# Set attention and a two-layer squared-ReLU network in one kernel: when a DMA may do an addition, when tokens are fetched, and rules for every four blocks

## The chip, the core and the metric

The kernel runs on one core of a Trainium2 chip. The metric is the device time of one execution in microseconds; less is better. TensorE (PE, with its weight loads shown apart as PEld), VectorE (DVE), ScalarE (ACT), GpSimd (POOL) and SyncE (SP, which here only issues DMAs) each run their own list of instructions in order and wait for one another by semaphores.

## What is computed

Four batches of 12480 tokens of width 128 attend to 32 inducing points, which have themselves attended to all tokens of their batch (`h`). The result goes through a network of width 2048 with `s * relu(h)^2 + b` between its layers.

```python
h = mab(I, x)                       # softmax(scale * I @ x.T) @ x, I is 32 x 128
x = mab(x, h).reshape(49920, 128)   # softmax(scale * x @ h.T) @ h
r = np.maximum(x @ w_in, 0.0)
return (s * (r * r) + b) @ w_out
```

## The kernel before, in words

Tokens stand in 104 blocks of 480 (26 for each of the four batches). A block passes through 8 pairs of hidden tiles (a pair is 2 x 128 hidden units, so its tiles are 128 x 960), which makes 832 pairs. A pair's work:

- PE: two matmuls h<-a2t,wst (`pair`, L988) of the block's attention weights with the weights that hold `h @ w_in`.
- ACT or DVE: r = relu(h) (L1000 on ACT, L1002 on DVE). The planner chooses.
- ACT: hi = the square of r, rounded to fp32r (`square`, L1062).
- PE: four matmuls of hi with w_lo and w_hi, summed into the block's output bank x (`out_part`, L1094).
- The rest that the rounding of hi lost, in one of three ways. **P**: DVE makes g = max(h,0)*r (L1031), POOL subtracts hi from it (L1042), and two matmuls with w_hi read that. **D**: DVE does both (L1031 into h, then L1042 on DVE). **Far**: DVE makes gm = -h*r (L1013), POOL issues a DMA that adds gm onto hi in memory (L1018; hi then has the home hm), and after it has landed two matmuls with w_neg = -w_hi read the sum. The four matmuls of hi must have read hm before that DMA may write it, and POOL waits for them.

So every pair costs PE the same eight matmuls, whichever way it goes.

Beside the pairs run chains of other steps, each beside a given block: `attend` (the attention of four blocks of tokens; one every fourth block, L838 to L876; it uses the output bank that the next block but one will need), and, except in the last batch, `scores`, `top` and `values` for the next batch's `h`. `attend` writes hl, from which SP's DMAs spread a2t for each block (L941). The tokens come in tiles xt of two blocks, two tiles to a group of four blocks, five buffers (`load_xt`, L359). `fetch` gives each load the block whose predecessor's output must have been made before it is issued (its gate, "ob"); both tiles of a group have had the same gate, two blocks ahead of their use (AHEAD = 2).

The order on every engine is written before the program runs, by a list scheduler (`Plan`). Each step has an engine or a choice of engines, a duration that the planner assumes, events that it waits for, and an urgency (the number of its pair, plus an offset from the rules: M_U for the first matmuls, R_U for the relu, OUT for the last matmuls, and so on); when engines come free, the step with the least start time plus WEIGHT times urgency is next. The durations are the planner's own: a far addition is taken to have landed M_LAND after POOL's issue, and a subtraction to take POOL_L on POOL. A pair goes far when this holds (M_PAIR is pairs 0 and 1 of a block, M_ROOM the two buffers of gm and hm):

```python
far = pr in (M_PAIR if steady else M_PAIR[:1]) and fars.get(k // NPAIR, 0) < M_MOST and blk_open(k)
far = far and max(next_free("gm", M_ROOM), next_free("hm", M_ROOM)) <= plan.end
```

`blk_open` asks whether the chain beside the block before has ended (in the plan) and the block before that has been written out; beside an attention it is mostly false when pairs 0 and 1 come. There are two sets of rules, `Opening` for pairs 0 to 15 and `Steady` for the rest, and `Steady` adds small offsets by the block's number in its batch and by pair.

Of the kernel before, what the change touches and what calls it, by code (L numbers as in the profile page):

```python
# [23 lines left out]
SB = 2  # L24
GR = 4
# [5 lines left out]
POOL_M = 0.6  # L31
M_LAND = 8.0
M_PAIR = (0, 1)
M_ROOM = 2
M_MOST = 1
G = 3
# [6 lines left out]
LAT = 0.195  # L43
IDLE = 0
BACK = 0.13
# [6 lines left out]
SETTLED = 16  # L52
END = 5
END_Q = 0.337
W_IN_U = -100
# [4 lines left out]
FRONT_0 = -9.51  # L60
# [22 lines left out]

class Opening:
    WEIGHT = 0.0229
    SLIP = 0.0865
    LEAN = {"ACT": -0.624}
    R_LEAN = {"DVE": 0.022}
    M_U = -8.4567
    R_U = 5.0037  # L90
    SQ = 2.0571
    S_U = -1.5635
    C_U = -15.3862
    OUT_HI = 2.8109
    OUT = 2.7863
    FRONT = -1.9358
    POOL_Q = 2.4761


class Steady:  # L100
    WEIGHT = 0.0178
    SLIP = 0.006
    LEAN = {'ACT': -0.624}
    R_LEAN = {'DVE': 0.021}
    M_U = -9.7754
    R_U = 4.4418
    SQ = 3.602
    S_U = -1.7977
    C_U = -16.8378
    OUT_HI = 2.732  # L110
    OUT = 2.166
    FRONT = -1.0039
    POOL_Q = 2.8611
    R_AT = [0.07, 0.0, 0.0, 0.0, 0.0, 0.0, 0.0, 0.0, 0.0, 0.0, 0.0, 0.02, 0.0, 0.0, 0.0, 0.0, -0.03, 0.0, 0.0, 0.0, 0.0, 0.0, -0.06, -0.0, 0.0, 0.0]
    Q_AT = [-0.01, 0.0, 0.0, 0.0, 0.0, 0.0, 0.16, 0.11, 0.01, 0.56, 0.17, 0.0, -0.18, 0.0, 0.58, 0.15, 0.0, 0.08, 0.0, -0.09, 0.0, 0.0, 0.0, 0.0, 0.0, 0.0]
    F_AT = [0.39, 0.0, 0.0, -0.12, 0.0, 0.0, 0.58, 0.0, -1.14, 1.46, 0.47, 0.52, 0.0, 0.0, 0.0, 0.0, -1.24, 0.0, 0.0, 0.0, -0.94, 0.0, 0.0, 0.0, 0.33, -0.95]
    R_PR = [0.03, 0.0, 0.0, -0.05, 0.01, 0.0, -0.07, 0.0]
    Q_PR = [-0.39, 0.53, 0.25, 0.19, 0.04, 0.0, 0.16, -0.35]

# [29 lines left out]
class Plan:  # L149
# [7 lines left out]
    def __init__(self):  # L157
        self.free, self.events, self.units, self.end, self.start = {}, Events(), [], 0.0, 0.0
        self.events[LOCK] = -math.inf
        self.pair_until = 0.0  # L160
        self.rules, self.lag = Opening, LAT

# [34 lines left out]
    def run(self):  # L197
        ev = self.events
        while self.units:
# [22 lines left out]
            self.units.remove(u)  # L222
            idle = self.eng == "PE" and self.rules is Steady and at > self.free.get("PE", 0.0) + 1e-6
            self.start, self.end = at, at + u[3][self.eng] + IDLE * idle
# [7 lines left out]
def tile_attn_relu2(ctx: ExitStack, tc: tile.TileContext, xT, xN, xF, indT, w_in, w_out, s_rep, b_rep, outT):  # L232
# [494 lines left out]
    def scores(b, g, ps, *waits):  # L727
# [17 lines left out]
        for q in range(nb):  # L745
            xt, turn = xt_tiles[b, (GR * g + q) // SB, 1]
            nc.tensor.matmul(ps[M * q:M * (q + 1), 0:BLK], ind_sb, xt[:, q % SB], start=True, stop=True)  # L747
            if q % SB == SB - 1:
                plan.set(turn)
        yield "DVE", 0.63  # L750
        nc.vector.tensor_tensor_reduce(
# [18 lines left out]
    def values(b, g, ps, *waits):  # L770
        d = st[b]
        rows = M * blocks_in(g)
        e = d["s"][0:rows, g]
        yield "ACT", 0.675, ("top", b), *waits
        nc.scalar.activation(
# [17 lines left out]
        plan.set(("eT", e_turn))  # L793
        yield "DVE", 0.29
        if g == 0:
# [179 lines left out]
    def pair(k):  # L975

        b, blk, pr = place(k)
        if k == SETTLED:
            plan.rules = Steady
        c, steady = plan.rules, plan.rules is Steady  # L980
        turn, free = ring("h", 3)
# [10 lines left out]
        if k + 1 < total:  # L992
            plan.spawn(pair(k + 1), k + 1, plan.end)
        lean = {"DVE": c.R_LEAN["DVE"] + c.R_AT[blk] + c.R_PR[pr]} if steady else c.R_LEAN
        yield dict(ACT=0.852, DVE=1.066), lean, c.R_U, room("r", RB)
# [8 lines left out]
        hi = {}  # L1004
        far = pr in (M_PAIR if steady else M_PAIR[:1]) and fars.get(k // NPAIR, 0) < M_MOST and blk_open(k)
        far = far and max(next_free("gm", M_ROOM), next_free("hm", M_ROOM)) <= plan.end
# [18 lines left out]
        wait = max(0.0, pool_work[0] - plan.end)  # L1025
        most = c.POOL_Q + (c.Q_AT[blk] + c.Q_PR[pr] if steady else 0.0) if k < total - END else END_Q
        kind = "P" if wait < most and next_free("g", G) <= plan.start else "D"
# [90 lines left out]
    def front_work(blk_g):  # L1118

        units = todo.pop(blk_g, [])  # L1120

        def ps():
            return bank[(blk_g + 1) % 2]

        def chain():
            first = True
            for f, args in units:
                for want in f(*args, ps):
                    yield (*want, ("ob", blk_g - 1), ("front", blk_g - 1)) if first and blk_g else want
                    first = False  # L1130
            plan.set(("front", blk_g))

        plan.spawn(chain(), blk_g * NPAIR + plan.rules.FRONT + (Steady.F_AT[blk_g % NBLK] if plan.rules is Steady else 0.0) if blk_g else FRONT_0, plan.end)

# [10 lines left out]
    for b in range(B):  # L1145
# [8 lines left out]
        for n, f, *args in sorted(units, key=lambda x: (x[0], rank.index(x[1]), x[2:])):  # L1154
            beside(at + n, f, *args)
            if f in (scores, attend):
                for j in range(args[1] * GR // SB, min(NSB, (args[1] + 1) * GR // SB)):
                    fetch(at + n - AHEAD, load_xt, args[0], j, 1 if f is scores else 2)
            elif f is values:
                for half in range(-(-TB // TH)):  # L1160
                    fetch(at + n - AHEAD, load_xn, *args, half)

# [32 lines left out]
    def opening():  # L1195
# [3 lines left out]
        for n, j in enumerate(order):  # L1199
# [13 lines left out]
            for c in [c for c, after in enumerate(W_AFTER) if after == n]:  # L1213
                yield from load_weight((), ("w_in", "w_out")[c // (F // WC)], c % (F // WC))
        for at, f, args in loads:
            yield from f([("ob", at - 1)] if at else [], *args)
# [94 lines left out]
```

## Time and profile before

| what | value |
|---|---|
| median of 3 runs | 1523.31 us (1523.16 to 1525.87) |
| profiled execution, its own time | 1526.3 us |
| its span from first to last instruction | 1524.5 us |
| granted TensorE clock, mean | 0.998 |
| busy PE / PEld | 1502.2 / 1298.3 us |
| busy DVE / ACT / POOL | 1435.1 / 1474.3 / 1454.6 us |
| far additions | 72 |

Matmuls are pipelined, and the profile models their ends, so a gap shorter than the part in which one matmul overlaps the next does not show as idle time of PE; PEld shows it. Each group of waits in the profile is put down to the engine whose event came last.

### The profile page before, as it was taken

To read this page: it belongs to the slowest core of one execution; us is meant where nothing else is said; L and a number is where in the kernel's file an instruction comes from. 1 tells how busy PE (TensorE), PEld (TensorE's weight loads), DVE (VectorE), ACT (ScalarE), POOL (GpSimd) and SP (SyncE) were. 2 spreads that over 40 slices of the span, in tenths; PEclk is the share of its full clock that TensorE was granted. 3 is DMA by queue.
4 is the path that set the end of the run, shared out by engine and by line. 5 is a ranking of instruction groups with operands and counts; after the bars stand their busy time and mean duration, and the time that the engine had idled before them with its cause. 6 is when DMAs were issued, how large, how long until landed. Compare 5 with 4: busy or idle time off the path is not lost.

```text
span 1524.5 us, 25228 instructions
## 1 busy us (share of the span) xinstructions
PE 1502.2 (99%) x8215; PEld 1298.3 (85%) x8215; DVE 1435.1 (94%) x1586; ACT 1474.3 (97%) x1779; POOL 1454.6 (95%) x714
## 2 busy tenths in 40 slices
PE   7899999999999999999999999999999999999998
PEld 5588888888888888888888888888888888888887
DVE  5899999999999999999999999999999999999998
ACT  6899999999999999999999999999999999999998
POOL 1599999999999999999999999999999999999998
PEclk9999999999999999999999999999999999999999
DMA  8244525425254343443435443534423233233322
GB/s 319 80 119 117 135 73 156 130 70 130 70 149 136 102 132 86 130 130 82 110 103 143 125 110 104 150 98 104 113 75 87 66 91 97 53 85 97 82 57 51
DMA packets 69922, 165.64 MB, mean 109 GB/s; under 512 B 13088, under 2 KB 39712, under 8 KB 69792
## 3 DMA queue, kind: packets, MB, share of 16 engines
q1 hardware_dynamic: 59280, 128.51, 27.1%
q0 software_dynamic: 10368, 35.39, 12.7%
q8 instruction: 67, 1.10, 0.3%
q14 instruction: 63, 0.52, 0.1%
q10 hardware_dynamic: 144, 0.12, 0.0%
HBM read 74.56 MB, written 25.56 MB: 66 GB/s over the span
## 4 chain that ended last, share of the span: by engine, by line
PE 81%; DVE 5%; POOL 5%; ACT 5%; issue 4%; DMA 0%; SPq 0%; DVEq 0%; ACTq 0%; POOLq 0%
PE x L1094 55%; PE h L988 19%; POOL g L1042 4%; DVE g L1031 3%; ACT g L1062 2%; ACT r L1000 2%; PE x L838 1%; PE x L787 1%; PE x L747 1%; PE x L527 1%; PE h L588 0%; PE h L553 0%; POOL hm L1018 0%; DMA gm<-in_xT_dram 0%; DVE r L1002 0%
## 5 line engine op out<-in xcount | busy, mean ns | idle before, releaser
L1042 POOL TENSOR_TENSOR g<-g,g 128x960 fp32r<-128x960 f32 x627 | 1415.8, 2580 | 17.8 <-DVE g L1031 9.6
L1094 PE MATMUL x<-g,w_hi 128*128 128x480 f32 x3040 | 959.9, 368 | 2.3 <-POOL g L1042 1.9
L1062 ACT ACTIVATE g<-r 128x960 fp32r<-128x960 f32 x760 | 737.4, 1009 | 12.1 <-PE x L1094 3.0
L1031 DVE SCALAR_TENSOR_TENSOR g<-h,r 128x960 f32<-128x960 f32 x627 | 706.5, 1147 | 31.4 <-ACT r L1000 20.2
L1000 ACT ACTIVATE r<-h 128x960 f32<-128x960 f32 x658 | 619.4, 971 | 10.0 <-PE h L988 6.9
L1094 PEld LDWEIGHTS x<-g,w_hi 128*128 128x128 f32 x3040 | 569.7, 189 | 61.3 <-POOL g L1042 10.7
L1094 PE MATMUL x<-g,w_lo 128*128 128x480 f32 x1520 | 559.0, 368 | 1.1 <-ACT g L1062 1.1
L988 PE MATMUL h<-a2t,wst 128*128 128x480 f32 x1664 | 484.2, 373 | 6.3 <-DVE g L1031 5.8
L988 PEld LDWEIGHTS h<-a2t,wst 128*128 128x128 f32 x1664 | 301.1, 189 | 78.6 <-issue 23.9
L1094 PEld LDWEIGHTS x<-g,w_lo 128*128 128x128 f32 x1520 | 288.1, 190 | 25.7 <-ACT g L1062 3.2
L1002 DVE TENSOR_SCALAR r<-h 128x960 f32<-128x960 f32 x174 | 199.8, 1150 | 9.9 <-PE h L988 8.2
L1042 DVE TENSOR_TENSOR g<-h,g 128x960 fp32r<-128x960 f32 x133 | 153.1, 1151 | 7.5 <-ACT g L1062 2.7
L1031 DVE SCALAR_TENSOR_TENSOR h<-h,r 128x960 f32<-128x960 f32 x133 | 153.7, 1156 | 0.8 <-ACT r L1000 0.2
L1013 DVE SCALAR_TENSOR_TENSOR gm<-h,r 128x960 f32<-128x960 f32 x72 | 82.8, 1150 | 3.8 <-ACT r L1000 3.7
L1018 POOL DMA_DIRECT2D hm<-gm x72 | 77.7, 1079 | 0.2 <-issue 0.2
L1062 ACT ACTIVATE hm<-r 128x960 fp32r<-128x960 f32 x72 | 72.7, 1009 | 1.0 <-DVE r L1002 0.2
L1107 ACT ACTIVATE ob<-x,bias 128x480 f32<-128x480 f32 x103 | 68.3, 664 | 2.1 <-PE x L1094 1.2
L1094 PE MATMUL x<-hm,w_lo 128*128 128x480 f32 x144 | 53.2, 369 | 0.0
L1094 PE MATMUL x<-hm,w_hi 128*128 128x480 f32 x144 | 52.8, 366 | 0.0
L1094 PE MATMUL x<-hm,w_neg 128*128 128x480 f32 x144 | 41.1, 367 | 0.0
L430 POOL TENSOR_TENSOR wst<-wst,g 128x512 f32<-128x512 f32 x4 | 5.2, 1305 | 30.5 <-DVE wst L427 27.0
L1094 PEld LDWEIGHTS x<-hm,w_lo 128*128 128x128 f32 x144 | 27.3, 189 | 5.1 <-issue 3.2
(151 smaller groups left out, 576.6 us busy)
## 6 DMA issues: line engine op xcount, KB each, us to landing
xt<-in_xT_dram SPq DMA_DIRECT2D x96, 480.0 KB, 5.3
hm<-gm POOLq DMA_DIRECT2D x72, 480.0 KB, 5.3
a2t<-hl SPq DMA_DIRECT2D x412, 60.0 KB, 2.0
out_dram<-ob SPq DMA_DIRECT2D x103, 240.0 KB, 2.0
xn<-in_xN_dram SPq DMA_DIRECT2D x18, 512.0 KB, 3.9
xn<-in_xN_dram SPq DMA_DIRECT2D x18, 448.0 KB, 4.3
wst<-whl SPq DMA_DIRECT2D x48, 64.0 KB, 2.0
g<-in_w_in_dram SPq DMA_DIRECT2D x4, 512.0 KB, 9.8
```

The lines of the kernel that those rows point to most:

```text
L527: nc.tensor.transpose(ps[0:T, q * P:(q + 1) * P], xt[:, a, q, :], ident)
L747: nc.tensor.matmul(ps[M * q:M * (q + 1), 0:BLK], ind_sb, xt[:, q % SB], start=True, stop=True)
L988: nc.tensor.matmul(h[:, u, 0:BLK], wst[:, n * P:(n + 1) * P], by_turns(A), start=True, stop=True)
L1000: nc.scalar.activation(out=r, in_=hv, func=AF.Relu)
L1002: nc.vector.tensor_scalar(out=r, in0=hv, scalar1=0.0, scalar2=None, op0=ALU.max)
L1013: nc.vector.scalar_tensor_tensor(out=gm, in0=hv, scalar=-1.0, in1=r, op0=ALU.mult, op1=ALU.mult)
L1018: nc.gpsimd.dma_start(out=hi["t"].bitcast(F32).rearrange("p u t -> p (u t)"), in_=gm.rearrange("p u t -> p (u t)"), accum_op=ALU.add,)
L1031: nc.vector.scalar_tensor_tensor(out=g, in0=hv, scalar=0.0, in1=r, op0=ALU.max, op1=ALU.mult)
L1042: eng.tensor_tensor(out=g2, in0=g, in1=hi["t"].bitcast(F32), op=ALU.subtract)
L1062: nc.scalar.activation(out=hi["t"], in_=r, func=AF.Square)
L1094: nc.tensor.matmul(o, w, by_turns(g), start=first and n == 0, stop=left == 0 and n == len(ops) - 1)
L1107: nc.scalar.activation(out=ob, in_=o, func=AF.Identity, bias=bias, scale=1.0)
```

## The change

Six things change; the diff is cut to them, and of the table of 26 rules two lines stand here.

1. Rules: one set for pairs 0 to 15 (with the values of before), and one for every four blocks (32 pairs) after that. The offsets by block and pair are gone.
2. FARS and OPEN replace M_MOST and the fixed `blk_open`: after pair 15 a pair may go far also beside an attention that has not ended, except where OPEN is 1 (the opening and one of the 26 sets). FARS is 1, and 2 in one set.
3. M_LAND goes from 8.0 to 8.5.
4. The second tile of a group of tokens, and the second half of an xn load, get a gate one block later than the first. Loads are then put in the order of their gates.
5. Three assumed durations fall (0.63 to 0.58, 0.675 to 0.59, 0.29 to 0.21 in `scores` and `values`).
6. END_Q, which lets POOL take subtractions of the last five pairs, goes from 0.337 to 0.5.

```diff
-M_LAND = 8.0
+M_LAND = 8.5
-M_MOST = 1
-END_Q = 0.337
+END_Q = 0.5
...
-class Opening:
...
-class Steady:
...
+SPAN = 4 * 8
+OPENING = Rules(0.0229, 0.0865, -0.624, 0.022, -8.4567, 5.0037, 2.0571, -1.5635, -15.3862, 2.8109, 2.7863, -1.9358, 2.4761, 1, 1)
+STEADY = [
+    Rules(0.0166, 0.2181, -0.624, 0.022, -7.777, 5.0037, 2.0571, -1.5635, -15.3862, 2.8109, 2.7198, -1.9358, 3.4453, 1, 0),
...
+def rules_at(k):
+    return OPENING if k < SETTLED else STEADY[min((k - SETTLED) // SPAN, len(STEADY) - 1)]
...
-        far = pr in (M_PAIR if steady else M_PAIR[:1]) and fars.get(k // NPAIR, 0) < M_MOST and blk_open(k)
+        far = pr in (M_PAIR if steady else M_PAIR[:1]) and fars.get(k // NPAIR, 0) < c.FARS and (not c.OPEN or blk_open(k))
...
-        most = c.POOL_Q + (c.Q_AT[blk] + c.Q_PR[pr] if steady else 0.0) if k < total - END else END_Q
+        most = c.POOL_Q if k < total - END else END_Q
...
             if f in (scores, attend):
-                for j in range(args[1] * GR // SB, min(NSB, (args[1] + 1) * GR // SB)):
-                    fetch(at + n - AHEAD, load_xt, args[0], j, 1 if f is scores else 2)
+                first = args[1] * GR // SB
+                for j in range(first, min(NSB, (args[1] + 1) * GR // SB)):
+                    fetch(at + n - AHEAD + j - first, load_xt, args[0], j, 1 if f is scores else 2)
             elif f is values:
                 for half in range(-(-TB // TH)):
-                    fetch(at + n - AHEAD, load_xn, *args, half)
+                    fetch(at + n - AHEAD + half, load_xn, *args, half)
...
-        for at, f, args in loads:
+        for at, f, args in sorted(loads, key=lambda x: x[0]):
```

What the scheduler makes of it, counted over the whole program (before, now): far additions 72, 100; subtractions on POOL 627, 608; pairs that DVE does alone 133, 124; relus on ACT 658, 650, and on DVE 174, 182; outputs ob (a block's bank plus the bias) copied by ACT 103, 94, and by DVE 0, 9. PE has the same 6656 matmuls for the pairs, and the same others. Of these counts the last 26 blocks (the last batch) have: far 20, 26; subtractions on POOL 151, 148; D 37, 34; relus on DVE 44, 46; ob on DVE 0, 3. On PE the two orders agree up to the first matmuls of pair 16.

The first place is DVE beside the attention of block 10, from its row sums to the next gm (x_86 is the bank with the attention, `s,mx<-x_85` a step of `scores`). Before:

```order
L856 TENSOR_REDUCE x_86<-x_86 128x15
L859 TENSOR_SCALAR x_86<-x_86 128x15
L863 RECIPROCAL l_1831<-x_86 128x15
L866 TENSOR_TENSOR x_86<-x_86,l_1831 128x480
L869 STREAM_TRANSPOSE x_86<-x_86 128x480
L1031 SCALAR_TENSOR_TENSOR g<-h,r 128x960 x2
L876 TENSOR_TENSOR hl<-x_86,hl 128x480
L1031 SCALAR_TENSOR_TENSOR g<-h,r 128x960 x2
```

and with the change (line numbers are 11 higher in `attend`, 10 in `pair`):

```order
L867 TENSOR_REDUCE x_86<-x_86 128x15
L870 TENSOR_SCALAR x_86<-x_86 128x15
L1041 SCALAR_TENSOR_TENSOR g<-h,r 128x960
L874 RECIPROCAL l_1816<-x_86 128x15
L877 TENSOR_TENSOR x_86<-x_86,l_1816 128x480
L880 STREAM_TRANSPOSE x_86<-x_86 128x480
L1023 SCALAR_TENSOR_TENSOR gm<-h,r 128x960
L887 TENSOR_TENSOR hl<-x_86,hl 128x480
```

One g has become a gm ahead of the attention's last step, so a far addition runs beside the attention's end; before, blocks 10 and 11 had none, and POOL did 19 subtractions between two additions.

The second place is SP, beside the last values that the second batch needs (64 x 1024 is the short last xn). Before:

```order
L941 DMA a2t<-hl 32x480 x4
L383 DMA xn<-in_xN_dram 64x1024
L383 DMA xn<-in_xN_dram 64x896
L359 DMA xt<-in_xT_dram 128x960 x2
L1110 DMA out_dram<-ob 128x480 x2
```

and with the change:

```order
L952 DMA a2t<-hl 32x480 x4
L394 DMA xn<-in_xN_dram 64x1024
L394 DMA xn<-in_xN_dram 64x896
L370 DMA xt<-in_xT_dram 128x960
L1120 DMA out_dram<-ob 128x480
L370 DMA xt<-in_xT_dram 128x960
L1120 DMA out_dram<-ob 128x480
```

The two tiles of tokens now stand on either side of a block's output.

## Rows read from the trace of the kernel before

**Rows 1.** The page: busy time and its share of the span, instructions, by engine.

```profile
PE 1502.2 (99%) x8215; PEld 1298.3 (85%) x8215; DVE 1435.1 (94%) x1586; ACT 1474.3 (97%) x1779; POOL 1454.6 (95%) x714
```

**Rows 2.** The page: the chain of work that ended last, shares of the span by engine.

```profile
PE 81%; DVE 5%; POOL 5%; ACT 5%; issue 4%; DMA 0%; SPq 0%; DVEq 0%; ACTq 0%; POOLq 0%
```

**Rows 3.** One piece of that chain in order of time (start us, us, what).

```profile
76.92 2.43 PE x L1094 x12
```

**Rows 4.** Busy time of each engine in two stretches: from the settling of the opening to the end of the third batch, and the last batch (start:end, length, busy us and instructions of each engine, granted clock, DMA share, GB/s).

```profile
85.00:1130.00 1045.00, 1043.14 (x5722) 908.68 (x5721) 1001.77 (x1097) 1025.23 (x1221) 1035.11 (x502) 1.00 0.42 114
1130.00:1500.00 370.00, 365.73 (x1777) 321.88 (x1775) 354.44 (x361) 365.89 (x427) 365.87 (x180) 1.00 0.31 77
```

**Rows 5.** Waits of the weight loads in 85 to 1130 us (who waited <- for whom: us in total, times, longest).

```profile
PEld h L988 <- DVE g L1031: 10.2, 22, 0.8
...
PEld x L1094 <- POOL g L1042: 4.4, 12, 0.8
...
PEld h L988 <- DVE r L1002: 2.4, 3, 0.8
```

**Rows 6.** The same in 1130 to 1500 us.

```profile
PEld h L988 <- DVE g L1031: 6.0, 12, 1.7
PEld x L1094 <- POOL g L1042: 5.7, 14, 1.5
...
PEld x L1094 <- DVE hl L876: 1.0, 4, 0.3
PEld x L1094 <- ACT g L1062: 1.0, 4, 0.3
```

**Rows 7.** The page's groups of instructions: line, engine, operation, out<-in, shapes, count | busy us, mean ns of one | idle before.

```profile
L1000 ACT ACTIVATE r<-h 128x960 f32<-128x960 f32 x658 | 619.4, 971 | 10.0 <-PE h L988 6.9
...
L1094 PEld LDWEIGHTS x<-g,w_lo 128*128 128x128 f32 x1520 | 288.1, 190 | 25.7 <-ACT g L1062 3.2
L1002 DVE TENSOR_SCALAR r<-h 128x960 f32<-128x960 f32 x174 | 199.8, 1150 | 9.9 <-PE h L988 8.2
L1042 DVE TENSOR_TENSOR g<-h,g 128x960 fp32r<-128x960 f32 x133 | 153.1, 1151 | 7.5 <-ACT g L1062 2.7
...
L1107 ACT ACTIVATE ob<-x,bias 128x480 f32<-128x480 f32 x103 | 68.3, 664 | 2.1 <-PE x L1094 1.2
```

**Rows 8.** POOL in order of time around the attention of block 10 (start us, us, engine line operation, count).

```profile
195.52 0.85 POOL L1018 DMA_DIRECT2D hm<-gm  x1
196.13 41.98 POOL L1042 TENSOR_TENSOR g<-g,g 128x960 fp32r<-128x960 f32 x19
237.95 0.99 POOL L1018 DMA_DIRECT2D hm<-gm  x1
```

**Rows 9.** Busy time of the engines beside that attention (columns as in Rows 4).

```profile
209.00:223.50 14.50, 14.50 (x76) 12.45 (x75) 14.01 (x19) 13.01 (x18) 14.50 (x8) 1.00 0.10 36
```

**Rows 10.** The line of DVE's last step of an attention (engine, operation, count: duration ns min/median/max, first and last start), the nearest row to a copy of ob on DVE.

```profile
L876 DVE TENSOR_TENSOR hl<-x,hl x28: 629/640/659, 66.3 to 1481.4; 128x480 fp32r<-128x480 f32 x24, 64x480 fp32r<-64x480 f32 x4
```

**Rows 11.** DVE's longest waits in 85 to 1500 us.

```profile
DVE g L1031 <- ACT r L1000: 19.9, 41, 1.5
...
DVE g L1031 <- POOL g L1042: 4.4, 15, 0.7
```

**Rows 12.** The line of the far addition over the whole span: durations as in Rows 10, who waited for it (us, times), and from issue to landing.

```profile
L1018 POOL DMA_DIRECT2D hm<-gm x72: 796/1012/1709, 96.3 to 1510.8; - x72
...
  PEld x L1094: 0.2, 1
...
DMA to landing us min/median/max: 4.3/5.3/9.6
```

**Rows 13.** The same line in 408 to 530 us, where the third batch's scores and the second batch's attentions need two tiles of tokens in nearly every block.

```profile
L1018 POOL DMA_DIRECT2D hm<-gm x7: 841/973/1523, 420.9 to 518.6; - x7
...
DMA to landing us min/median/max: 5.9/7.2/9.1
```

**Rows 14.** The same line in 1150 to 1480 us, in the last batch, where tokens come for one attention in four blocks.

```profile
L1018 POOL DMA_DIRECT2D hm<-gm x19: 796/872/1471, 1155.5 to 1467.8; - x19
...
DMA to landing us min/median/max: 4.4/4.7/7.7
```

**Rows 15.** One far addition in order of time (columns as in Rows 8).

```profile
461.65 0.89 POOL L1018 DMA_DIRECT2D hm<-gm  x1
```

**Rows 16.** The matmuls that read it, by the tile w_neg in 465 to 475 us: durations, first and last start, and what ended the wait before them.

```profile
L1094 PE MATMUL x<-hm,w_neg x2: 367/419/471, 470.6 to 470.9; 128*128 128x480 f32 x2
...
  DMA hm<-gm: 0.2, 1
```

**Rows 17.** The tile of tokens in 240 to 270 us: its use in an attention, its two loads, and their landing.

```profile
L838 PE MATMUL x<-xt,hT x8: 566/578/591, 266.8 to 267.2; 128*32 128x480 f32 x8
L359 SPq DMA_DIRECT2D xt<-in_xT_dram x2: 423/424/424, 244.4 to 244.8; - x2
...
DMA to landing us min/median/max: 6.4/6.8/7.1
```

**Rows 18.** The tile xn in 250 to 262 us: loads that had the next block's gate.

```profile
L383 SPq DMA_DIRECT2D xn<-in_xN_dram x2: 328/350/372, 255.7 to 256.1; - x2
```

**Rows 19.** Busy time at the end of the program (columns as in Rows 4).

```profile
1500.00:1524.50 24.50, 20.43 (x97) 17.66 (x96) 19.00 (x18) 18.14 (x22) 18.83 (x10) 0.97 0.24 54
```

More of the change, by code (lines that the diff above doesn't have):

```diff
@@ L43 @@
 LAT = 0.195
-IDLE = 0
+IDLE = 0.0
 BACK = 0.13
@@ L81, with __init__ @@
 AHEAD = 2
-class Opening:
[L85 to L97, printed above, removed]
-class Steady:
[L101 to L118, printed above, removed]
+class Rules:
+    NAMES = (
+        "WEIGHT", "SLIP", "ACT", "RELU", "M_U", "R_U", "SQ", "S_U", "C_U", "OUT_HI", "OUT", "FRONT", "POOL_Q",
+        "FARS", "OPEN",
+    )
+    def __init__(self, *values):
+        for name, value in zip(self.NAMES, values):
+            setattr(self, name, value)
+        self.LEAN = {"ACT": self.ACT}
@@ L160, in __init__ @@
         self.pair_until = 0.0
-        self.rules, self.lag = Opening, LAT
+        self.rules, self.lag = OPENING, LAT
     def spawn(self, unit, urgency=0.0, ready=0.0):
@@ L222, in run @@
             self.units.remove(u)
-            idle = self.eng == "PE" and self.rules is Steady and at > self.free.get("PE", 0.0) + 1e-6
+            idle = self.eng == "PE" and self.rules is not OPENING and at > self.free.get("PE", 0.0) + 1e-6
             self.start, self.end = at, at + u[3][self.eng] + IDLE * idle
@@ L749, in scores @@
                 plan.set(turn)
-        yield "DVE", 0.63
+        yield "DVE", 0.58
         nc.vector.tensor_tensor_reduce(
@@ L773, in values @@
         e = d["s"][0:rows, g]
-        yield "ACT", 0.675, ("top", b), *waits
+        yield "ACT", 0.59, ("top", b), *waits
         nc.scalar.activation(
@@ L793, in values @@
         plan.set(("eT", e_turn))
-        yield "DVE", 0.29
+        yield "DVE", 0.21
         if g == 0:
@@ L977, in pair @@
         b, blk, pr = place(k)
-        if k == SETTLED:
-            plan.rules = Steady
-        c, steady = plan.rules, plan.rules is Steady
+        c = plan.rules = rules_at(k)
+        steady = k >= SETTLED
         turn, free = ring("h", 3)
@@ L993, in pair @@
             plan.spawn(pair(k + 1), k + 1, plan.end)
-        lean = {"DVE": c.R_LEAN["DVE"] + c.R_AT[blk] + c.R_PR[pr]} if steady else c.R_LEAN
+        lean = {"DVE": c.RELU}
         yield dict(ACT=0.852, DVE=1.066), lean, c.R_U, room("r", RB)
@@ L1131, in chain @@
             plan.set(("front", blk_g))
-        plan.spawn(chain(), blk_g * NPAIR + plan.rules.FRONT + (Steady.F_AT[blk_g % NBLK] if plan.rules is Steady else 0.0) if blk_g else FRONT_0, plan.end)
+        plan.spawn(chain(), blk_g * NPAIR + plan.rules.FRONT if blk_g else FRONT_0, plan.end)
     def beside(blk_g, f, *args):
```

26 lines of the change are left out of this document (added).

## The prediction, made before the changed kernel was run

> **What bounds the kernel now.** I read the page's busy shares first. PE is busy 99% of the span, ACT 97%, POOL 95% and DVE 94% [rows 1]: nothing is far from full, so the shares alone don't name the bound. The chain that ended last lies on PE for 81% and on DVE, POOL and ACT for 5% each [rows 2]: PE is the floor, and the others stop it now and then. Its best pace is 12 matmuls in 2.43 us, 0.2025 us each [rows 3]; none of the pairs' matmuls is added or removed, so this floor doesn't move. The change can only give back PE's waits, or add some.
>
> So the second look is by stage. Up to 1130 us, PE is idle 1.9 us of 1045 by the busy view, and POOL, with 1035, is nearly as full. In the last batch PE is idle 4.3 us of 370, while POOL and ACT are both busy 365.9 of 370 and DVE 354.4 [rows 4]: there is no work for a next batch there, PE has less to do for each block, and the three elementwise engines together set the pace. These are two different limits, and one unit of saved work isn't worth the same in both.
>
> The third look is at the waits of the weight loads, since a busy PE hides short gaps. A load takes 0.190 us [rows 7] and runs one slot of 0.2025 us ahead, so I count a late load as costing its wait less 0.2 us. Up to 1130 us the waits for DVE, POOL and DVE's relu are 10.2 + 4.4 + 2.4 = 17.0 us in 37 [rows 5]; less 37 x 0.2 that is **9.6 us** at most. In the last batch they are 6.0 + 5.7 + 1.0 + 1.0 = 13.7 us in 34 [rows 6], less 6.8, **6.9 us**. So some 16 us is all that the orders after 85 us can return; the lower bounds, from the idle of PE itself, are 1.9 and 4.3 [rows 4].
>
> **The change part by part.** *More far additions: 72 become 100.* First what each kind of step occupies. POOL's 19 subtractions without an addition took 41.98 us, 2.21 each; and from the start of a far addition's issue to the next subtraction it was 196.13 - 195.52 = 0.61 us [rows 8]. So 19 fewer subtractions and 28 more issues take 19 x 2.21 - 28 x 0.61 = 42.0 - 17.1 = **24.9 us off POOL**. DVE's first step is one for each pair in all three ways, so its number stays. DVE's own subtractions fall by 9 of 1.151, its relus rise by 8 of 1.150 [rows 7], and it gets 9 copies of ob. No row has that copy on DVE; the bounds are 0.64, a DVE step of the same 128 x 480 from the same bank [rows 10], and 0.664, the copy itself on ACT [rows 7], and I take the former, as it is the same engine's. DVE: -10.4 + 9.2 + 5.8 = **+4.6**. ACT loses 8 relus of 0.971 and 9 copies of 0.664 [rows 7]: **-13.7**. Together -34.0.
>
> Of that the last batch has: POOL -3 x 2.21 + 6 x 0.61 = -3.0; DVE -3 x 1.151 + 2 x 1.150 + 3 x 0.64 = +0.8; ACT -2 x 0.971 - 3 x 0.664 = -3.9; sum -6.1. There the three engines share the work, the planner may shift relus and subtractions between them, and all were near full, so a third of it reaches the end: **-2.0 us** (bounds: 0 if the saved work lands in idle time, -6.9 if all waits go).
>
> The rest, -27.9, falls before 1130 us. A third would be 9.3 us, but there PE is the limit and only its waits can go. Beside the attention of block 10 POOL was busy 14.50 of 14.50 us, without one far addition, and so was PE [rows 9]: full POOL alone doesn't stop PE. Of the 9.6 us, POOL's part is 4.4 - 12 x 0.2 = 2.0; POOL's 10 idle us there become some 32, so I let all of it go. DVE's part is 12.6 - 25 x 0.2 = 7.6; DVE itself stands mostly waiting for ACT's relu, 19.9 us in 41 waits [rows 11]; ACT is eased by 1% but DVE has no less to do, and I let a third go, 2.5. Sum **-4.5 us** (bounds: 0, if the waits only move; -9.6).
>
> What would end PE's waits is a choice for every four blocks instead of one set of rules; but no row shows a plan's mistakes, so I give **the new rules themselves** nothing beyond the waits above, from 0 to the rest of the 16.5 us; their loss side is the rival below.
>
> *The landing.* The two w_neg matmuls wait for it in PE's fixed order: if it is late, everything behind them on PE waits. An addition takes 4.3 to 9.6 us to land, 5.3 in the median, and PE waited for it 0.2 us once in 72 [rows 12]; that was the one issued at 461.65 and read at 470.6, 9.0 us later [rows 15, 16]. The planned landing now is 0.5 us later, which adds room. Alone a landing takes 4.4 to 4.7; beside two token loads the median is 7.2 and the longest 9.1 [rows 13, 14]. For 100 additions: **+0.3 us** (100/72 of 0.2), bounds 0 and 28 x (9.6 - 9.0) = 17 if every added one landed like the slowest.
>
> On the DMA's sharing the Trainium skill ("DMA: Bandwidth & Descriptors", SWDGE vs HWDGE vs iDMA) says that each engine takes turns between the queues of software and hardware descriptors. By that, an addition beside loads could take about twice its 4.4 us alone, an estimate of 8.8, PE would never have waited, and the term would be 0; the trace has 9.6 and 9.1, so its own rows are used.
>
> *The second tile one block later.* Costed at 0, with this cover: the two loads at 244.4 and 244.8 landed at most 7.1 us after issue and were read at 266.8 [rows 17]. A load with the next block's gate went at 255.7 [rows 18]; with the same landing it is there at 262.8, 4.0 us before its use. Where loads come densest, their buffers and not the gate hold them, and nothing changes. SP issues as many DMAs as before; a load that waits for its buffer now stands between two outputs, with outputs and a2t behind it. If that cover fails, attention and a2t slip; one late attention costs PE what it is late.
>
> *Opening, end and durations.* The opening keeps its values and PE's order to pair 16: 0. The end has the same kinds of pairs in the last eight, w_neg now stands ahead of the last four matmuls instead of last, and PE was idle 4.1 of the last 24.5 us, mostly after its last matmul [rows 19]: 0, within 1 us. The three shorter assumed durations act through the order alone.
>
> **Sum:** -2.0 - 4.5 + 0.3 = -6.2. Against the profiled execution, 1526.3, that gives 1520.1. That execution lay 3.0 above the median of the runs, 1523.31; the same step from there gives **1517.1 us**.
>
> **The rivals.** *A, the elementwise engines bind everywhere.* Then a third of all 34.0 us comes off, -11.3 + 0.3 = -11.0: 1512.3. For it: POOL is busy 1035 of 1045 us up to 1130 too [rows 4], and the additions now go exactly under the attentions, where DVE and POOL were fullest [rows 9]. Against: PE is fuller still. The Trainium skill ("Perfetto Trace Analysis", Identifying the Most-Contended Engine) says that matmul busy time is no good measure of TensorE's nearness to its limit and that the share of weight loads is to be read instead; that share is 87% here [rows 4], and by it PE would have room everywhere and A would be the forecast. The trace's own slot speaks against so much room: at best pace loads fill only 0.190 of 0.2025, 94%. Chance 0.13.
>
> *B, the waits only change their place.* The order is fixed by assumed durations; new waits arise where real ones differ, as before. Then stage one returns nothing, the last batch 2.0 or less: about 1521.5, within 0.2% (3.0 us, about what a measurement of this kernel can tell from no change). For it: the waits of the weight loads are many and short, 0.8 us at the longest up to 1130 [rows 5], which looks like jitter around a plan rather than a plan with holes; and DVE has 4.6 us more to do. That the change doesn't do what it says is excluded, as the order has the 100 additions. Chance 0.23.
>
> *C, slower: landings pass their reading.* Place: w_neg on PE, in the ten blocks of a batch with two loads each, three batches, so about 30 of the 100 additions. There the median was 7.2 with fewer additions [rows 13]; now each block has one, on top of the loads. If half of the 30 come as late as the slowest, 0.7 us past the 9.0 at which the earliest is read, PE loses 10.5 us: 1523.3 - 6.2 + 10.5 = 1527.6. It decides from 13 such waits: 13 x 0.7 = 6.2 + 3.0. Against it: 0.2 us in 72 so far [rows 12], and the half microsecond more. Chance 0.16, with other ways to be slower of the same size (an order with new holes) in it.
>
> **How the numbers follow.** The forecast, a gain of 3 to 9 us, has 0.48, A 0.13, B 0.23, C 0.16. Faster: 0.48 + 0.13 = 0.61. Within 0.2%: 0.23. Slower: 0.16. The likeliest case alone spans 1514 to 1520. The range takes in A with its bound in the waits (down to 1509.5, 14 of the 16.5 us) and B, and reaches into C to 1527; about 0.07 lies above and 0.05 below.
>
> **What would show it.** Right: POOL's busy time falls by some 20 us or more, ACT's by about 14, PE's stays; the waits of weight loads for POOL almost vanish up to 1130 us; PE's idle in the last batch falls below 3 us; the span shortens about twice as much before the last batch as in it. For A: the stage before shortens by 9 us. For B: PE's waits for DVE's g keep their sum. For C: w_neg appears among those who wait for a DMA, with more than 9 us in all. Wrong altogether: a2t or tiles of tokens among PE's releasers, or PE's first 17 pairs taking another time.

## The result, and the profile after

The changed kernel takes **1531.74 us** in the median of 5 runs (1530.78 to 1535.02), against 1523.31: a ratio of 1.0057, 95% interval 1.0043 to 1.0072. It is slower by 8.4 us, where 6.2 less were forecast. The profiled execution took 1531.1 us.

The two traces are compared by stage first. Blocks begin where PE starts the h<-a2t,wst matmuls of their first pair; "104" stands for the end of the last pair's, after which 6.2 us follow to PE's last matmul in both kernels. The times are worked out from those starts, the differences before rounding; the last column is from PE's last matmul to the end.

| us | before block 2 | blocks 2 to 78 | blocks 78 to 104 | last matmul to end |
|---|---|---|---|---|
| before | 85.9 | 1073.3 | 355.2 | 4.0 |
| changed | 82.9 | 1076.2 | 358.0 | 6.1 |
| difference | -3.0 | +2.9 | +2.9 | +2.1 |

What lies ahead of the first pair varies from one execution to another (first pair at 52.4 to 56.0 us over the profiles here, with blocks 0 to 2 at 30.1 in all of them), so the first column says nothing on the change. The other three make 7.9 of the 8.4 us. In sixteen stretches of six or eight blocks (2 to 10, 10 to 16 and so on) the changed kernel is ahead by up to 3.4 us in six and behind by up to 3.4 in ten.

The page after, busy time by engine and the chain, answers to [rows 1, 2]:

```profile
PE 1501.1 (98%) x8215; PEld 1296.7 (85%) x8215; DVE 1440.9 (94%) x1594; ACT 1469.2 (96%) x1762; POOL 1439.2 (94%) x723
...
PE 83%; POOL 5%; DVE 4%; ACT 3%; issue 3%; DMA 1%; SPq 0%; DVEq 0%; ACTq 0%; POOLq 0%
PE x L1104 57%; PE h L998 20%; POOL g L1052 5%; DVE g L1041 2%; PE x L849 1%; PE x L798 1%; PE x L758 1%; DMA a2t<-hl 1%; ACT r L1010 1%; ACT g L1072 1%; POOL hm L1028 1%; PE x L538 0%; PE h L599 0%; DMA g<-in_w_in_dram 0%; ACT hm L1072 0%
...
L1052 POOL TENSOR_TENSOR g<-g,g 128x960 fp32r<-128x960 f32 x608 | 1387.1, 2626 | 29.2 <-DVE g L1041 16.3
...
L1010 ACT ACTIVATE r<-h 128x960 f32<-128x960 f32 x650 | 614.2, 969 | 17.4 <-PE h L998 13.3
```

Work did leave the elementwise engines: POOL -15.4 us, ACT -5.1, DVE +5.8, and PE's own time is the same within 1.1. (Busy time counts overlapping records once: in [rows 7] 658 relus of 971 ns make 638.9 us of work and 619.4 of busy time, here 650 of 969 ns make 629.9 and 614.2. So it fell by less than the steps did.) Yet the end came later, and a transfer, a2t<-hl, stands in the chain. Two stretches answer to [rows 4]:

```profile
85.00:1130.00 1045.00, 1042.38 (x5715) 906.93 (x5714) 1004.40 (x1102) 1020.98 (x1208) 1018.35 (x507) 1.00 0.49 125
1130.00:1500.00 370.00, 362.23 (x1756) 318.15 (x1755) 353.00 (x359) 360.74 (x419) 361.04 (x180) 1.00 0.35 83
```

PE's idle in the last batch rose from 4.3 to 7.8 us, at the same granted clock of 1.00. The waits of weight loads, first in 85 to 1130 us, then in 1130 to 1500, answer to [rows 5, 6]:

```profile
PEld h L998 <- issue: 23.2, 48, 0.8
...
PEld h L998 <- DVE g L1041: 7.0, 11, 0.8
PEld x L1104 <- POOL g L1052: 6.7, 26, 0.5
```

```profile
PEld x L1104 <- POOL g L1052: 8.9, 25, 0.9
PEld h L998 <- issue: 8.0, 13, 2.2
PEld h L998 <- DVE g L1041: 5.0, 9, 1.6
```

The waits for DVE's g fell (22 to 11, 12 to 9; 10.2 to 7.0 us in the first stretch), but those for POOL's g rose from 12 to 26 and from 14 to 25, though POOL has 19 subtractions less. And PE itself has a line that the kernel before has not (longest waits of PE over the whole span):

```profile
PE h L998 <- DVE g L1041: 5.5, 7, 2.3
PE h L998 <- DMA a2t<-hl: 4.4, 3, 1.8
```

**The collision.** The three waits lie at the first pairs of blocks 12, 82 and 98: 0.9, 1.7 and 1.8 us. In order of time at block 82 (start us, us, engine, line, operation):

```profile
1208.85 8.64 SPq L952 DMA_DIRECT2D a2t<-hl  x12
...
1210.06 0.94 POOL L1028 DMA_DIRECT2D hm<-gm  x1
...
1215.77 0.64 PE L998 MATMUL h<-a2t,wst 128*128 128x480 f32 x2 [1.66 <-DMA a2t<-hl]
```

The attention has ended, SP spreads its hl into the a2t of three blocks, four 60 KB transfers each, and 1.2 us later POOL issues an addition of 480 KB. The first block's four, by their line in 1208.8 to 1211 us:

```profile
L952 SPq DMA_DIRECT2D a2t<-hl x4: 513/562/582, 1208.9 to 1210.7; - x4
...
  PE h L998: 1.7, 1
...
DMA to landing us min/median/max: 1.9/2.0/4.9
```

Three of four landed in about 2 us, the last took 4.9, and PE read it as soon as it came. From the first issue to the last landing such a block takes 3.8 us in the kernel before at blocks 82, 90 and 98, and it then had 1.6 to 1.8 us to spare; now it takes 6.8, 6.0 and 7.2, with 0.1 to 0.2 to spare. Over the program the median landing of a2t went from 2.0 to 2.8 us while that of the additions stayed (5.3, 5.4):

```profile
hm<-gm POOLq DMA_DIRECT2D x100, 480.0 KB, 5.4
...
a2t<-hl SPq DMA_DIRECT2D x412, 60.0 KB, 2.8
```

On two queues that share the engines, the Trainium skill ("DMA: Bandwidth & Descriptors", SWDGE vs HWDGE vs iDMA) says that each engine goes round between them. By that, a2t could take about twice its 3.8 us beside an addition, an estimate of 7.6; the trace's 6.0 to 7.2 lies a little below it. The prediction turned this rule on the addition's landing alone.

**The end.** PE's last matmul is followed by 6.1 us in place of 4.0. What comes last there is a DRAIN on POOL, an instruction that is not counted as busy. It is in the answer on the line at the kernel's end, for POOL alone: of before, then of the changed kernel (min/median/max ns, first and last start).

```profile
L1304 POOLq DRAIN  x3: 34/93/6072, 1517.0 to 1524.3; - x3
```

```profile
L1315 POOLq DRAIN  x3: 34/102/9392, 1519.2 to 1529.1; - x3
```

The longest of each begins beside POOL's last subtractions. It ends 3.80 us after the last of them before, and 6.09 now. Half a microsecond of the later end is the order's: POOL's last subtraction ended 1.31 us before PE's last matmul did, and now ends 0.80 before it. In all runs with 79 additions or more the program ends 0.8 us after this DRAIN. SP's waits in the last 30 us show who feels it (the kernel before has 0.6, 2, 0.5 there):

```profile
SPq L1315 <- PEq L1315: 2.7, 2, 2.3
...
SPq L1315 <- DMA out_dram<-ob: 1.2, 2, 0.9
```

### The profile page after: what moved, and what is told of

It is laid out like the page before. It is cut to its first block, busy times and chain, and to the rows that moved or that the text cites. A ratio compares the mean times of both kernels' runs of the same rounds, so it can differ in the third digit from the quotient of the medians.

```text
span 1529.3 us, 25200 instructions
## 1 busy us (share of the span) xinstructions
PE 1501.1 (98%) x8215; PEld 1296.7 (85%) x8215; DVE 1440.9 (94%) x1594; ACT 1469.2 (96%) x1762; POOL 1439.2 (94%) x723
## 4 chain that ended last, share of the span: by engine, by line
PE 83%; POOL 5%; DVE 4%; ACT 3%; issue 3%; DMA 1%; SPq 0%; DVEq 0%; ACTq 0%; POOLq 0%
PE x L1104 57%; PE h L998 20%; POOL g L1052 5%; DVE g L1041 2%; PE x L849 1%; PE x L798 1%; PE x L758 1%; DMA a2t<-hl 1%; ACT r L1010 1%; ACT g L1072 1%; POOL hm L1028 1%; PE x L538 0%; PE h L599 0%; DMA g<-in_w_in_dram 0%; ACT hm L1072 0%
## 5 line engine op out<-in xcount | busy, mean ns | idle before, releaser
L1052 POOL TENSOR_TENSOR g<-g,g 128x960 fp32r<-128x960 f32 x608 | 1387.1, 2626 | 29.2 <-DVE g L1041 16.3
L1104 PE MATMUL x<-g,w_hi 128*128 128x480 f32 x2928 | 927.5, 369 | 2.0 <-POOL g L1052 0.9
L1072 ACT ACTIVATE g<-r 128x960 fp32r<-128x960 f32 x732 | 710.6, 1006 | 14.5 <-DVE r L1012 1.3
L1010 ACT ACTIVATE r<-h 128x960 f32<-128x960 f32 x650 | 614.2, 969 | 17.4 <-PE h L998 13.3
L1104 PEld LDWEIGHTS x<-g,w_hi 128*128 128x128 f32 x2928 | 547.9, 189 | 64.7 <-POOL g L1052 16.3
L1104 PE MATMUL x<-g,w_lo 128*128 128x480 f32 x1464 | 537.7, 367 | 0.0
L1023 DVE SCALAR_TENSOR_TENSOR gm<-h,r 128x960 f32<-128x960 f32 x100 | 114.7, 1147 | 4.8 <-ACT r L1010 4.6
L1028 POOL DMA_DIRECT2D hm<-gm x100 | 105.7, 1057 | 10.4 <-ACT g L1072 3.1
L1072 ACT ACTIVATE hm<-r 128x960 fp32r<-128x960 f32 x100 | 100.7, 1007 | 0.9
L1104 PE MATMUL x<-hm,w_lo 128*128 128x480 f32 x200 | 73.9, 370 | 0.2 <-DVE hl L887 0.2
L1104 PEld LDWEIGHTS x<-hm,w_neg 128*128 128x128 f32 x200 | 37.8, 189 | 2.7
```

The costliest lines, as they stand in the source:

```text
L1010: nc.scalar.activation(out=r, in_=hv, func=AF.Relu)
L1023: nc.vector.scalar_tensor_tensor(out=gm, in0=hv, scalar=-1.0, in1=r, op0=ALU.mult, op1=ALU.mult)
L1028: nc.gpsimd.dma_start(out=hi["t"].bitcast(F32).rearrange("p u t -> p (u t)"), in_=gm.rearrange("p u t -> p (u t)"), accum_op=ALU.add,)
L1052: eng.tensor_tensor(out=g2, in0=g, in1=hi["t"].bitcast(F32), op=ALU.subtract)
L1072: nc.scalar.activation(out=hi["t"], in_=r, func=AF.Square)
L1104: nc.tensor.matmul(o, w, by_turns(g), start=first and n == 0, stop=left == 0 and n == len(ops) - 1)
```

## The experiments

The kernel before was run beside each set, at medians of 1524.0 to 1524.3 us; ratios are to it. The changed kernel was not timed again beside them: differences to its 1531.74 cross sessions, in which the kernel before moved by 0.7 to 1.0 us, so the profiles' stretches decide. "Steady" is the time of blocks 2 to 104 in the profile, which leaves out the varying opening; for comparison, before 1428.4, changed 1434.2. Two profiles with the same order on an undisturbed stretch agree there within 0.1 us.

**The size of the additions.** In the changed kernel each addition moves a quarter (128 x 240 of 128 x 960); what is left out is the rest of the correction.

```diff
-                out=hi["t"].bitcast(F32).rearrange("p u t -> p (u t)"),
-                in_=gm.rearrange("p u t -> p (u t)"), accum_op=ALU.add,
+                out=hi["t"][:, 0, 0:BLK // 2].bitcast(F32),
+                in_=gm[:, 0, 0:BLK // 2], accum_op=ALU.add,
```

> The changed kernel in its own order, but each far addition moves only the first 240 of its 1920 columns' half tiles (128 x 240 instead of 128 x 960); the rest of gm is not added. Theory 1 (an addition issued beside an attention's end shares the DMA engines with the a2t transfers, which land late: 5.99 to 7.15 us for blocks 82, 90 and 98 against 3.8 before, and PE stands for them, 4.4 us in 3 waits): a2t of these blocks lands within 4.5 us, PE's waits for it vanish, and the time falls from 1531.7 by 4 to 6 us, to about 1527. Theory 2 (the new rules alone order the work worse): bytes don't matter, 1530 to 1533.

Measured: 1522.31 us, 0.9989 [0.9980, 0.9997]; steady 1424.9, the a2t waits gone from PE's list, a2t's median landing back at 2.0. So 9.4 us of the changed kernel's time (9.3 by steady) are the size of 100 additions, more than either theory had expected, and the order as such, with such small additions, is a shade better than before's. The tail stayed at 6.05. The control is the same edit in the kernel before, 72 quarter additions:

> The kernel before in its own order, with each of its 72 additions moving 128 x 240 instead of 128 x 960; the rest of gm is not added. It is the control for the changed kernel with such small additions, which was 9.4 us faster than with whole ones. Theory 1 (the cost comes of additions beside an attention, which the kernel before has hardly any of): within 2 us of 1524. If additions cost their bytes wherever they stand: 5 to 7 us faster, 1517 to 1519.

1524.22, 1.0003 [0.9994, 1.0011], beside 1524.32 with full ones. No time comes back there; steady is even 1.0 longer, all of it in blocks 58 to 64, where PE waits 0.7 us for block 64's a2t though no addition was issued within 6 us of it (what held it up was not found). So what costs is where an addition stands, not that it moves 480 KB.

**The same bytes a little later.** The additions of six blocks (11, 45, 49, 81, 89, 97) are issued one POOL subtraction, some 2.2 us, later; no other engine's order changes.

```diff
+            if k // NPAIR in LATER:
+                later.append(issue)
+            else:
+                issue()
...
+        if kind == "P":
+            while later:
+                later.pop()()
```

> The changed kernel, except that in six blocks (11, 45, 49, 81, 89, 97) the far addition stands one subtraction later on POOL; these are the six whose a2t landed only 0.13 to 0.25 us before PE read it, with the addition issued 0.6 to 1.6 us after the first a2t transfer. All other engines keep their order, all bytes are moved. Theory 1 (these collisions cost the time that PE stood for a2t, 4.4 us in three waits, and what follows from them): a2t of these blocks lands 1 to 2.5 us sooner after its issue, PE's waits for a2t vanish, and the time falls by 4 to 5.5 us to about 1527. If bytes everywhere count (all of the 9.4 us that smaller additions gave back): at most 2 us faster, 1530 or more.

1528.32, 1.0028 [1.0016, 1.0039]; steady 1428.8, 5.4 less than the changed kernel. By stretches it returns 1.1 us in blocks 10 to 16, 1.9 in 78 to 84 and 2.1 in 96 to 104, where the waits of 0.9, 1.7 and 1.8 stood, and 0.4 in 84 to 90. The same place in its trace, SP's line in 1208 to 1210.2 us, and then POOL in order of time:

```profile
L953 SPq DMA_DIRECT2D a2t<-hl x4: 513/560/582, 1208.2 to 1210.0; - x4
...
DMA to landing us min/median/max: 1.9/2.0/2.0
```

```profile
1211.58 0.95 POOL L1031 DMA_DIRECT2D hm<-gm  x1
```

All four land in 2.0 us, and the addition comes 3.4 us after the first of them. No byte was taken away; the collision is shown. (The six subtractions also come 0.6 us sooner for it, but the quarter additions, with POOL's order untouched, gave the same 1.1 and 1.9 us back in the first two of these stretches.) Then the additions of 19 blocks, all those next to an attention's end:

> The changed kernel, with the far addition of 19 blocks (11, 15, 19, 23, 29, 37, 41, 45, 49, 55, 59, 67, 71, 81, 85, 89, 93, 97, 101) issued by POOL one subtraction later; every other engine has the changed kernel's order. If the collisions of additions with a2t after an attention are what the size of the additions costs (9.4 us between the changed kernel and its quarter-size twin), and if moving six of them returned 3 to 5 us, moving all of them should return more: 1524 to 1527, about 2 below the 1528.3 of six. Rival, the rest of the 9.4 us is not a2t: no more than six returned, 1528. Second rival, an addition that goes some 2.8 us later lands after its planned reading at some places: w_neg among those who wait for a DMA, and 1529 to 1531.

1526.85, 1.0018 [1.0009, 1.0027], which overlaps the interval with six; steady 1429.0, so no more than with six. It gains 1.0 us in blocks 22 to 34 and loses 0.7 in 34 to 40, where PE now waits 0.6 us for block 37's addition: issued at 588.43, read at 596.5. The rest of what size costs (1428.8 against 1424.9) is spread over many stretches by up to 0.8 us each; what carries it was not found.

**The loads.** Both tiles, and both halves of xn, get the old gate. First in the changed kernel, then with additions later at blocks 11, 15, 45, 49, 81, 89 and 97, then with all 19 later:

```diff
-                    fetch(at + n - AHEAD + j - first, load_xt, args[0], j, 1 if f is scores else 2)
+                    fetch(at + n - AHEAD, load_xt, args[0], j, 1 if f is scores else 2)
...
-                    fetch(at + n - AHEAD + half, load_xn, *args, half)
+                    fetch(at + n - AHEAD, load_xn, *args, half)
```

> The changed kernel with both tiles of a group at the old gate (only the order of loads on SP differs; PE, DVE, ACT and POOL have the same order). Theory 1 and theory 2: no change, 1531.7 within 1.5 us, since no load was read less than 3.6 us after its landing. Theory 3 (the moved loads now collide with a2t or additions): 2 to 5 us faster.

> The same with seven blocks (15 also) and both tiles of a group at the old gate. If the old gate's 2.2 us and the six collisions are separate costs, 1524.5 to 1526; if the old gate only changed which a2t collided, the same as with the additions later alone.

> The same, and both tiles of a group with the old gate. If the loads' new gate costs 1.8 to 2.2 us as the two pairs of kernels so far say by their medians: 1522.5 to 1525, level with the kernel before. If that difference was only a collision at block 98 that the later addition has taken away already: the same as the kernel beside it within 0.5 us.

1529.54 (1.0034 [1.0022, 1.0047]), 1526.56 (1.0015 [1.0007, 1.0024]) and 1529.12 (1.0030 [1.0019, 1.0042]): against the kernel with the new gate (in the second without block 15's addition later) 2.2 less, 1.8 less, 2.3 more. The profiles say where. In the first, steady is 2.0 shorter, all of it in blocks 96 to 104: block 98's a2t took 5.0 us in place of 7.2, and PE's waits for a2t went from 4.4 in 3 to these:

```profile
PE h L998 <- DMA a2t<-hl: 2.4, 2, 1.6
```

In the second, steady is the same (1428.7 against 1428.8); the medians' 1.8, whose intervals overlap, has no place in the profile. In the third, steady is 3.1 longer, all in blocks 34 to 40. The tile w_neg in 570 to 600 us there:

```profile
L1115 PE MATMUL x<-hm,w_neg x4: 366/486/767, 582.2 to 598.8; 128*128 128x480 f32 x4
...
  DMA hm<-gm: 4.6, 2
```

PE itself stood 2.1 of these us. That is the prediction's rival C, at one addition here, at the same one in the kernel with all 19 later (0.6 us), and at one in the last experiment below, each time only after it had been put off by hand. So the gate has no sign of its own: it shifts transfers by a microsecond or two, and whether one then meets a late neighbour decides.

**One half of the plan without the other.** The rules and loads of the change, END_Q as before, and `blk_open` asked again everywhere (74 additions):

```diff
-        far = ... and fars.get(k // NPAIR, 0) < c.FARS and (not c.OPEN or blk_open(k))
+        far = ... and fars.get(k // NPAIR, 0) < c.FARS and blk_open(k)
```

> The changed kernel, with its new rules and loads, but no additions beside an attention that has not ended (74 additions). Theory 1: near the kernel before, 1522 to 1526, no waits for a2t. Theory 2: still slow, 1529 to 1533.

The rules of before with open additions and M_LAND 8.5 (102 additions):

```diff
-        far = ... and fars.get(k // NPAIR, 0) < M_MOST and blk_open(k)
+        far = ... and fars.get(k // NPAIR, 0) < M_MOST and (steady or blk_open(k))
```

> The kernel before, with its own rules, but additions allowed beside an attention and a landing of 8.5 in the plan (102 additions instead of 72). Theory 1: slower than before by 3 to 6 us, 1526 to 1529, with PE waiting for a2t. Theory 2: the additions help or do nothing, 1519 to 1524.

And the change with a single set of rules after pair 15:

```diff
-    return OPENING if k < SETTLED else STEADY[min((k - SETTLED) // SPAN, len(STEADY) - 1)]
+    return OPENING if k < SETTLED else STEADY[9]
```

> The changed kernel with one set of rules after pair 15 (the tenth of the 26) in place of one for every four blocks. All else is the changed kernel's: additions beside attentions (102 here), M_LAND, loads, durations. If the rules for every four blocks are what makes the plan fit the additions (additions alone with the old rules gave 1539.6): slower by 5 us or more, 1537 to 1545. If the choice for every four blocks is worth nothing: 1531.7 within 1.5.

Measured: 1535.57 (1.0072 [1.0059, 1.0084]), 1539.62 (1.0098 [1.0082, 1.0113]) and 1540.66 (1.0105 [1.0089, 1.0121]); steady 1438.5, 1442.4 and 1443.1. The first two are slower than either theory had expected, the third lies as expected. The rules without the additions cost 11.6 us, the additions without the rules 15.6, both together 8.4. The rules for every four blocks are worth 8.9 us beside these additions (by steady), and each of the two is a larger loss without the other. Not all of the second one's loss need be the order: a2t lands within 0.3 us of its reading in it at blocks 4, 12, 16, 50 and 82. M_LAND and the three assumed durations were not run apart. Most weight loads that wait in the last of the three still wait for nothing the profile shows, or for POOL (whole span, longest first; other engines' rows left out):

```profile
PEld h L998 <- issue: 33.3, 65, 0.9
...
PEld x L1104 <- POOL g L1052: 22.3, 62, 1.2
...
PEld h L998 <- DVE g L1041: 15.0, 25, 2.6
```

**No additions at all.** `far` is false throughout: 660 subtractions on POOL.

> The changed kernel with its rules and loads, but no far addition at all (POOL does 660 subtractions, DVE 172). For the end of the program: from the end of POOL's last subtraction to the end of its drain it was 3.80, 3.96, 6.09 and 6.25 us in kernels with 72, 74, 100 and 102 additions, 0.082 us more for each. If the number of additions sets it, the drain here ends within 0.5 us of the last subtraction; if it belongs to the end's order, 3 to 6 us. The whole should be slower by 15 us or more, as PE loses the steps that POOL no longer gives away.

1552.29 in one run, 28 us above the kernel before. So additions do relieve the elementwise engines by much. Under the changed rules the first 74 bring 16.7 us (1535.57, with the old END_Q) and the 26 beside attentions 3.8 more (1531.74), collisions and all. It also has the other end of the DRAIN: 2302 ns, begun with POOL's last subtraction and over 0.07 us after it.

```profile
L1315 POOLq DRAIN  x3: 34/78/2302, 1543.6 to 1550.0; - x3
```

**Only the last batch.** Kernel before up to block 78, then the changed rules, open additions and M_LAND, with the additions of blocks 81, 85, 89, 93, 97 and 101 later: an attempt at a version better than both.

```diff
+        last = k >= LAST * NPAIR
+        if last:
+            plan.rules = LATES[min((k - SETTLED) // 32, 25) - 19]
...
-            plan.spawn(landed(k, hi, m_turn), 0.0, plan.end + M_LAND)
+            plan.spawn(landed(k, hi, m_turn), 0.0, plan.end + (8.5 if last else M_LAND))
```

> The kernel before up to the end of the third batch, on every engine; from block 78 on the changed kernel's rules, open additions and M_LAND, with the additions of blocks 81, 85, 89, 93, 97 and 101 issued by POOL one subtraction later (79 additions in all; loads, assumed durations and END_Q as before). If the last batch has a gain of its own once additions don't meet a2t (353.6 in place of 355.2 us for blocks 78 to 104) and the end goes with the number of additions (79 x 0.082, less what 72 already hide: up to +0.4): blocks 78 to 104 in 353 to 354, the time 0.8 to 1.6 below the kernel before, about 1523 beside 1524.3. Rival, rules chosen for one order don't fit one that comes to block 78 in another state: 355 or more, 1524 to 1528.

1529.13, 1.0031 [1.0018, 1.0043]: slower even than the rival's 1524 to 1528, and in its direction. Blocks 78 to 104 took 360.3 us, where the same rules, reached from the changed kernel's state, with three of these additions later and with the changed kernel's loads and assumed durations, take 353.6. The loss is in blocks 84 to 96 (+5.9 against before). Those blocks' time, of before and of this kernel:

```profile
1240.00:1405.20 165.20, 162.19 (x792) 142.81 (x791) 157.51 (x159) 162.83 (x191) 162.95 (x81) 1.00 0.32 80
```

```profile
1238.50:1409.50 171.00, 167.13 (x797) 143.89 (x795) 159.93 (x161) 164.06 (x191) 158.68 (x81) 0.99 0.38 91
```

POOL stands idle 12.3 us there in place of 2.3, with the same 81 instructions, and no engine is fuller for the length: the order fits less well. PE also stands 1.3 us there for an addition: the edit issues two put-off ones at 1320.85 and 1321.43, and the second lands 7.6 us later, at 1329.05 (its line in the whole span):

```profile
PE x L1136 <- DMA hm<-gm: 1.3, 1, 1.3
```

How much of the loss is that one wait and how much the fit wasn't told apart. The end took 4.3 us with 79 additions, 0.35 more than before. A version that beats both kernels was not found.

## Why the prediction was wrong, point by point

- **The first three batches, -4.5 expected: failed.** Blocks 2 to 78 took 2.9 us more. 0.9 of it is the collision at block 12 and what followed; 2.0 stays with the additions later, and even with quarter additions only -0.7 is won. The step took PE's waits for POOL as POOL's load and let them go with it. POOL's occupancy did fall as costed (from start to next start a subtraction takes 2.20 us and an addition 0.61 in both traces), but it turned into idle time of POOL (14.0 us before and 35.6 now, between 85 and 1500 us), while PE's waits for it rose. My reading, which no run tests by itself, is that a wait in a fixed order is a matter of when one piece of work is placed against its reader, not of how full its engine is. Rival B described this stage, though not by its sign: the waits for DVE's g did not keep their sum, they fell from 10.2 to 7.0 us, and others took their place.
- **The last batch, -2.0: right in size under a loss that was not in the sum.** It took 2.9 more; with the collisions away 1.6 less, with quarter additions 2.8 less. That this stage is bound by the elementwise engines fits, though no run tests it alone; that the size came out so near is partly luck, as a third was a guess.
- **The additions' side effect: the missing term.** The prediction followed each added transfer to its own landing and reader (w_neg), and not to the transfers beside it. It showed in the order that the additions would stand at an attention's end, where hl goes out as a2t, and named a2t among what would prove it wrong, but only as a slip of the loads; it gave it no price. Price by the runs: 5.4 us, from three waits of 4.4 us and what they delayed. The spare time could be read beforehand: 1.4, 1.8 and 1.6 us between a2t's landing and its reading at blocks 12, 82 and 98 before.
- **The landing, +0.3: 0.** Landings were 4.4 to 9.4 us, and no w_neg waited. Rival C's time, 1527.6, was nearest, by another mechanism, and so by luck; its own showed in three experiments, at additions put off by hand.

The line of the addition over the whole span answers to [rows 12]:

```profile
L1028 POOL DMA_DIRECT2D hm<-gm x100: 841/992/1745, 93.3 to 1512.8; - x100
...
who waited for it (us, times):
...
DMA to landing us min/median/max: 4.4/5.4/9.4
```

Nobody stands under those who waited.

- **The second tile, 0: right as a direct cost,** 2.0 us by the collision at block 98 (part of the 5.4), as the three pairs of runs show.
- **The end, 0 within 1 us: failed,** +2.1. The prediction looked at the last pairs' work and not at what the program waits for after it.
- **The signs it named as right:** POOL's busy time fell by 15.4 us in place of 20, ACT's by 5.1 in place of 14, the waits for POOL rose, and PE's idle in the last batch went to 7.8 and not below 3. The first two are misread rather than missed: busy time counts overlapping records once, and the steps fell as planned.
- **Rival A,** the elementwise engines binding everywhere, is out: POOL's idle rose and the time did not fall. The share of weight loads, 87% before and after in 85 to 1130 us, did not tell how little room there was.

Together: +5.4 (collisions), +2.1 (the end) and +0.4 for the rest of the plan (+2.0 up to block 78, -1.6 after it) make the 7.9 us of the stages; the 0.5 up to 8.4 lies in the openings and the scatter of the runs, and isn't settled.

## What to carry to other kernels

When a DMA is added, list every other transfer in flight in its window and how long before its reading each lands; the small one with little to spare pays, not the large one that was planned with room. In an order that is fixed ahead, less load on an engine can become idle time of that engine, as POOL's did here, unless the waits themselves are placed anew, and rules tuned for one order can lose when a part of it, even a better part, is put in another. Read the program's last microseconds by every engine's closing instructions, not by the last piece of work.

## What the hardware showed that was not expected

POOL's closing DRAIN lasts longer the more additions POOL has issued, whatever their size. From POOL's last subtraction to its end: 0.07 us after no addition, 3.80 after 72 (full or quarter), 3.96 after 74, 4.37 after 79, 6.09 after 100 (full or quarter, early or late), 6.25 after 102. Beyond 72 that is 0.082 us for each. Up to 74 it is hidden behind the output's landing and SP's close, 3.2 us after the last matmul; at 79 it sets the program's end, 4.3 us after that matmul, at 100, 6.1. From 0 to 72 it is 0.052 on average, so the line isn't straight, and why the DRAIN follows the count is open.

A 480 KB addition is little disturbed by the 60 KB transfers that it holds up: its median landing moved from 5.3 to 5.4 us, while a2t's moved from 2.0 to 2.8, and a block's four took 6.0 to 7.2 us in place of 3.8 where the two met.
